# A two-layer decoder step on one core: another table of heads, kept caches and engine orders

## The chip, the core and the metric

The kernel runs on one core of one Trainium2 chip. The core has five engines that this text speaks of: PE (TensorE: matrix products), DVE (VectorE), ACT (ScalarE), POOL (GpSimd) and SP (SyncE, which here only issues DMA transfers). They run side by side and wait for each other by semaphores. The on-chip memory (SBUF) holds operands in 128 partitions; PE writes its sums into PSUM banks. The metric is the device time of one execution in microseconds (us), as the median of several runs.

## The reference

Two equal layers, each an attention block with residual and an FFN block with residual, for 4 tokens that each have their own K and V caches. Both layers use the same weights and the same caches.

```python
def _A_ref(x, k_cache, v_cache, wq, wo):          # B=4, D=448, Hq=16, Hkv=8, Dh=256, Sk=8192
    W = min(4096, max(256, Sk // 4))              # 2048: only the last 2048 positions
    q = (x @ wq).reshape(B, Sq, Hq, Dh).transpose(0, 2, 1, 3)
    k = jnp.repeat(k_cache[:, :, Sk - W:, :], rep, axis=1)      # rep = 2
    v = jnp.repeat(v_cache[:, :, Sk - W:, :], rep, axis=1)
    p = softmax(einsum("bhqd,bhkd->bhqk", q, k) * Dh ** -0.5)
    o = einsum("bhqk,bhkd->bhqd", p, v)
    return o.transpose(0, 2, 1, 3).reshape(B, Sq, Hq * Dh) @ wo
def _B_ref(x, w_gate, w_up, w_down):              # F = 1792
    return (silu(x @ w_gate) * (x @ w_up)) @ w_down

x = x + _A_ref(layernorm(x), ...)
x = x + _B_ref(layernorm(x), ...)
x = x + _A_ref(layernorm(x), ...)
x = x + _B_ref(layernorm(x), ...)
```

One token and one KV head ("a head" below) need 1 MB of K and 1 MB of V. The 32 heads of the 4 tokens are needed in layer 0 and again in layer 1, 64 heads in all. All data is bf16.

## The kernel before

**Slots and kept caches.** The weights are loaded once and stay. K and V go through 31 slots of 512 KB each, 7 more being the space of wq after its last use. A K takes two slots, a V comes in two halves with a slot each. Since both layers read the same caches, a K or a V half that the table `HOLD` names stays in its slots from layer 0 to layer 1 and is not loaded again: 21 K and 45 V halves. `SLOTS` says which slot each load takes. A load waits until the last reader of what was in its slot before has run.

**Heads and groups.** `PLAN` lists the order of the 64 heads, each as token, layer, head ("302" is token 3, layer 0, head 2). Items joined by a plus are one group of two heads, a blank parts stages, and an ampersand marks a group whose scores are made in another form (for two heads: each head's scores on their own). A group (`group`, L859) goes through: loads of K (L875 as one of 1 MB, where `WHOLE` names the head, or L881 as two halves) and of V (L897); a transpose of each K half on DVE (L887, only when the K has just been loaded); the expanded q on POOL (L926); scores on PE (L920); the maximum on DVE (L936), two small products on PE that spread it (L941, L944), its negative (L950); the exponential on ACT (L954); a turn of the probabilities on PE (L969) and their copy (L978); the totals (L986, L992); the products with V (L1001); scaling (L1015, L1017, L1019); a flip of the result (L1025, L1035). Two groups are in flight on most buffers.

**Out-projection, FFN and norm.** The out-projection (`out_proj`, L1039) adds each head to a sum in one PSUM bank, by rows (L1055, four matmuls) for all but the last head of a token and layer, and by columns (L1047) for the last; `rows` (L793: ACT copy L794, DVE subtract L796, PE turn L804, DVE add L808) brings the row sums into column form, and `residual` (L811) adds the column sums. After a token's last head come norm (L551), FFN and norm, and in layer 0 the token's q-projection for layer 1 (`qproj`, L598). The FFN has two forms. By columns (`ffn`, L711): 112 matmuls for gate and up (L740) and 56 for down (L776), each of 32 columns. By rows (`ffn_row`, L658): gate and up by L678, wide row operations (L684, L686, L688), a turn (L694) and down by rows into the sum's bank (L706), followed by `rows` again. `ROWF = (1, 2)` names the tokens that take rows in layer 0; tokens 0 and 3 take columns, and the FFN at the end of layer 1 takes columns for those tokens that have waited.

**What sets the order.** The engines' orders are written out by hand as lists of numbers (`SEQ_PE`, `SEQ_DVE`, `SEQ_ACT`, `SEQ_POOL`, `SEQ_SP`). `schedule` (L237) puts the operations into these orders, adds the waits that the data needs, and inserts zero matmuls (L1137 and, when no operand has to be loaded anew, L543), each a product with zero that adds nothing to a PSUM bank, where `SEQ_PE` has a "w" with a number. A zero matmul "w" goes into the bank of the row sums, between two of its readers. An engine that waits holds all that stands behind it in its order; this holds for SP's loads as well.

## Time and profile before

The median of 3 runs is 276.81 us (276.73 to 277.32).

| | |
|---|---|
| span of the profiled execution | 277.7 us (277.67) |
| PE busy | 242.4 us, 87% |
| DVE busy | 185.0 us, 67% |
| POOL busy | 80.4 us, 29% |
| ACT busy | 62.8 us, 23% |
| read from HBM | 100.77 MB, 363 GB/s over the span |
| mean granted clock of PE | 0.984 |

"Busy" counts instructions of the engine that work on data; a matmul and the load of its weights (PEld) overlap. The span is that of one profiled execution, from its first to its last instruction; the runs are timed without the profile. In a group of instructions, "mean ns" is the time of one record, which can overlap with the next, so that a group's busy time divided by its count is the cost of one. The chain of waits is followed back from the last instruction: a "DMA" piece is time in which the chain stood for a transfer.

### The profile page before, as it was taken

To read this page: it belongs to the slowest core of one execution; us is meant where nothing else is said; L and a number is where in the kernel's file an instruction comes from. 1 tells how busy PE (TensorE), PEld (TensorE's weight loads), DVE (VectorE), ACT (ScalarE), POOL (GpSimd) and SP (SyncE) were. 2 spreads that over 40 slices of the span, in tenths; PEclk is the share of its full clock that TensorE was granted. 3 is DMA by queue.
4 is the path that set the end of the run, shared out by engine and by line. 5 is a ranking of instruction groups with operands and counts; after the bars stand their busy time and mean duration, and the time that the engine had idled before them with its cause. 6 is when DMAs were issued, how large, how long until landed. Compare 5 with 4: busy or idle time off the path is not lost.

```text
span 277.7 us, 10576 instructions
## 1 busy us (share of the span) xinstructions
PE 242.4 (87%) x4751; PEld 126.5 (46%) x4576; DVE 185.0 (67%) x574; ACT 62.8 (23%) x173; POOL 80.4 (29%) x224
## 2 busy tenths in 40 slices
PE   3997999999999887998888887979799787989995
PEld 0121232233475553544445444535455456667664
DVE  4666817735612687978857599986768757389841
ACT  0003021111112222331332333224132321232411
POOL 1160121111024221615044243133234332254350
PEclk9998899999999999999999999999989999999998
DMA  7999999999999999999999999999999998799200
GB/s 278 425 420 413 415 395 418 399 401 406 405 387 417 411 412 414 410 409 411 351 394 400 414 417 411 408 413 408 358 384 350 411 378 297 279 396 411 81 2 3
DMA packets 25740, 101.44 MB, mean 365 GB/s; under 512 B 2523, under 2 KB 6623, under 8 KB 21471
## 3 DMA queue, kind: packets, MB, share of 16 engines
q1 hardware_dynamic: 25687, 100.78, 91.8%
q8 instruction: 36, 0.59, 0.9%
q14 instruction: 9, 0.07, 0.1%
q10 hardware_dynamic: 8, 0.00, 0.0%
HBM read 100.77 MB, written 0.00 MB: 363 GB/s over the span
## 4 chain that ended last, share of the span: by engine, by line
PE 40%; DMA 36%; DVE 14%; issue 3%; ACT 2%; SPq 2%; POOL 2%; DVEq 0%; ACTq 0%
DMA half<-in_A_v_cache_dram 24%; DMA half<-in_A_k_cache_dram 12%; DVE half L887 8%; PE S L920 8%; PE A L543 6%; PE Y L1001 6%; PE A L1137 5%; PE Z L740 3%; PE A L1055 2%; PE Z L776 2%; PE A L1047 1%; PE Y L969 1%; SPq L521 1%; DVE oh L1019 1%; SPq L897 1%
## 5 line engine op out<-in xcount | busy, mean ns | idle before, releaser
L887 DVE STREAM_TRANSPOSE half<-half 128x1024 uint32<-128x1024 uint32 x86 | 104.7, 1229 | 8.8 <-DMA half<-in_A_k_cache_dram 8.8
L1137 PE MATMUL A<-identb,small 128*128 128x512 bf16 x139 | 53.3, 389 | 3.3 <-DVE A L447 2.9
L1015 POOL TENSOR_TENSOR small<-small 128x2 f32<-128x2 f32 (+1 forms) x48 | 38.5, 805 | 47.1 <-DVE small L992 29.7
L543 PE MATMUL A<-identb,small 128*128 128x512 bf16 x175 | 51.8, 397 | 0.0
L920 PE MATMUL S<-half,qe 128*8 128x128 bf16 (+1 forms) x1520 | 45.0, 240 | 6.6 <-issue 2.8
L1001 PE MATMUL Y<-half,pT 128*8 128x256 bf16 (+1 forms) x1024 | 42.9, 274 | 8.4 <-DMA half<-in_A_v_cache_dram 5.0
L920 PEld LDWEIGHTS S<-half,qe 128*8 128x8 bf16 x1520 | 30.5, 84 | 22.3 <-DVE half L887 9.8
L954 ACT ACTIVATE praw<-S,small 104x128 bf16<-104x128 f32 (+2 forms) x48 | 19.4, 404 | 68.3 <-DVE small L950 64.1
L1019 DVE SCALAR_TENSOR_TENSOR oh<-oh,small,Y 128x256 bf16<-128x256 bf16 x48 | 22.5, 468 | 16.9 <-ACT oh L1017 16.7
L926 POOL TENSOR_TENSOR qe<-qc,tiny 128x64 bf16<-128x64 bf16 x64 | 18.1, 294 | 43.9 <-PE S L920 35.2
L1001 PEld LDWEIGHTS Y<-half,pT 128*8 128x8 bf16 (+1 forms) x1024 | 20.2, 84 | 23.0 <-DVE small L992 6.5
L1017 ACT ACTIVATE oh<-Y 128x256 bf16<-128x256 f32 x48 | 18.4, 383 | 45.8 <-PE Y L1001 37.3
L1137 PEld LDWEIGHTS A<-identb,small 128*128 128x128 bf16 x139 | 14.6, 105 | 14.9 <-issue 8.9
L577 POOL TENSOR_SCALAR st<-st 128x1 f32<-128x1 f32 x16 | 4.3, 267 | 57.6 <-DVE st L567 56.4
L978 ACT ACTIVATE pT<-Y 128x64 bf16<-128x64 f32 (+1 forms) x48 | 12.4, 258 | 36.0 <-PE Y L969 29.6
L1055 PE MATMUL A<-wo_sb,oT 128*4 128x448 bf16 x192 | 17.5, 356 | 2.0 <-issue 1.1
L1082 POOL MEMSET oT<- 128x16 bf16 x39 | 4.1, 112 | 38.4 <-PE A L1055 32.1
L992 DVE TENSOR_REDUCE small<-Y 128x2 f32<-128x32 f32 (+1 forms) x48 | 9.1, 189 | 8.8 <-PE Y L986 7.9
L1035 DVE TENSOR_TENSOR oT<-Y,small 128x4 bf16<-128x4 f32 (+1 forms) x63 | 9.0, 155 | 5.8 <-PE Y L1025 4.5
L950 DVE TENSOR_REDUCE small<-S 104x1 f32<-104x32 f32 (+1 forms) x48 | 8.5, 177 | 5.2 <-PE S L944 5.0
L941 PE MATMUL S<-small,identb 104*104 104x32 bf16 (+1 forms) x48 | 10.0, 208 | 1.9 <-DVE tiny L936 1.5
L1025 PEld LDWEIGHTS Y<-tiny,oh 128*128 128x128 bf16 x96 | 7.0, 98 | 9.6 <-DVE oh L1019 4.9
(139 smaller groups left out, 266.9 us busy)
## 6 DMA issues: line engine op xcount, KB each, us to landing
half<-in_A_v_cache_dram SPq DMA_DIRECT2D x83, 512.0 KB, 9.9
half<-in_A_k_cache_dram SPq DMA_DIRECT2D x30, 1024.0 KB, 11.2
half<-in_A_k_cache_dram SPq DMA_DIRECT2D x26, 512.0 KB, 8.9
wo_sb<-in_A_wo_dram SPq DMA_DIRECT2D x8, 448.0 KB, 17.2
half<-in_A_wq_dram SPq DMA_DIRECT2D x3, 1024.0 KB, 8.5
wd_sb<-in_B_w_down_dram SPq DMA_DIRECT2D x1, 1568.0 KB, 18.3
wg_sb<-in_B_w_gate_dram SPq DMA_DIRECT2D x1, 1344.0 KB, 18.0
wu_sb<-in_B_w_up_dram SPq DMA_DIRECT2D x1, 1344.0 KB, 20.8
```

The source lines that it names most:

```text
L543: return e.add_instruction(mybir.InstMatmult(start_tensor_calc=start, stop_tensor_calc=stop, ldweights=load, name=nc.get_next_instruction_ ...
L887: return e.transpose(a, a)
L920: last = e.matmul(Sb[s_][qd:qd + 8, 0:32 * 2 * J], lhsT=qe[q_][:, P, ce, :, :].rearrange("p a n -> p (a n)"), rhs=keys(kcs[P], J * x, J, c ...
L926: g.op(POOL, "qe", lambda e, P=P, t=t, kvh=kvh: e.tensor_tensor(qe[q_][:, P, :, :, :], qc[t][:, kvh, :, :].unsqueeze(2).broadcast_to([128, ...
L954: return e.activation(praw[0:R, 0:N].rearrange("p (g r l) -> p g r l", g=J, l=2), Sb[s_][0:R, 0:N].rearrange("p (l g r) -> p g r l", l=2, ...
L978: g.op(SCA, f"pt{n}", lambda e: e.activation(pf, Yb[p_][:, 0:PW], ACT.Copy), r=(f"yp{p_}",), w=(f"pT{pt}",), bank=(f"Y{p_}",))
L1001: last = e.matmul(Yb[p_][32 * gg:32 * gg + M, 256:512], lhsT=pT[pt][:, gg, 2 * a + hv, 4 * P:4 * P + M] if n == 2 else pf[:, 16 * gg + 8 * ...
L1015: g.op(POOL, f"pow{n}", lambda e: e.tensor_tensor(ri[p_][:, 0:2 * n], rs[p_][:, 0:2 * n], expo[:, 1:1 + 2 * n], op=ALU.pow), r=(f"rs{p_}", ...
L1017: g.op(SCA, "oh", lambda e: e.activation(oh[:, :], Yb[p_][:, 256:512], ACT.Copy), r=(f"y{p_}",), w=("oh",), bank=(f"Y{p_}",))
L1019: g.op(DVE, "oho", lambda e: e.scalar_tensor_tensor(out=oh[:, :], in0=oh[:, :], scalar=lomask[:, 0:1], in1=Yb[p_][:, 256:512], op0=ALU.mul ...
L1055: last = e.matmul(Ab[32 * k:32 * k + B, 0:D], lhsT=oT[oi][:, k % 2, k // 2, :], rhs=wo_sb[:, 4 * kvh + k, :], start=False, stop=False, ski ...
L1137: return e.matmul(Ab[:, 0:512], lhsT=w, rhs=rhs, start=False, stop=False, skip_group_check=True)
```

## The change

The tables are new, and three pieces of code with them.

- `HOLD` keeps 25 K and 44 V halves. SP issues 145 loads and one store where it issued 157 and one.
- `PLAN` has 46 stages and 55 groups (9 of two heads, 46 of one) where it had 38 and 48 (16 and 32). In layer 0 of a token, heads that are not kept come first and heads that are kept later; in layer 1 those that need a reload come at the end.
- 78 transposes instead of 86, 295 zero matmuls instead of 314. 10 of them stand behind the last matmul of the program.
- The FFN of token 1 in layer 0 is "mixed": gate and up by rows, down by columns. Tokens 0, 2 and 3 take columns (token 2 together with token 0 of layer 1). For this the down product by columns moves out of `ffn` into `ffn_down`, and `ffn_row` calls it when asked for a column result. No FFN makes its down product by rows any more, and `rows` is called 8 times instead of 10.
- Zero matmuls can go into a second bank, `Z2`: "z" with a number in `SEQ_PE`.

```diff
-ROWF = (1, 2)
+ROWF = ()
+MIXF = (1,)
 PLAN = (
-    "005+001", "002+000", "006", "007", "003+004", "101 102", "100", "017+015", "016&014", "107 013", "103 105",
...
+    "006 001", "004", "005&007", "002 003&", "000&", "100 101", "015", "013&", "016+012", "014&", "103&", "104",
...
+    "215&", "110 111", "317", "312+315", "310+313", "314+316", "211+311", "210",
 HOLD = (
...
+    "k00 k02 v020 v021 k03 v030 v031 k04 v040 v041 k05 v050 v051 k06 v060 v061 k07 v070 v071 k12 v121 k13 v130 v131 "
...
-    def schedule(self, filler):
+    def schedule(self, filler, filler2):
         real = len(self.ops)
         inA = [o for o in self.ops if o.eng != PE and "A" in o.bank]
+        inZ, on_pe = [], True
+        for o in self.ops:
+            if "Z2" in o.bank:
+                if o.eng != PE and on_pe:
+                    inZ.append([])
+                if o.eng != PE:
+                    inZ[-1].append(o)
+                on_pe = o.eng == PE
+        inZ = inZ[[z[0].kind for z in inZ].index("qc"):]
...
-                if x[0] == "w":
+                if x[0] == "z":
+                    o, k = Op(len(self.ops), PE, "fw", filler2), int(x[1:])
+                    for d in inZ[k]:
+                        o.deps[d] = True
+                    for d in inZ[k + 1] if k + 1 < len(inZ) else ():
+                        d.deps[o] = True
+                    self.ops.append(o)
...
-        def ffn_row(ts):
+        def ffn_row(ts, column=False):
...
+            if column:
+                return ffn_down(ts, lambda fc: hT[:, 16 * (fc % 4) + 4 * (fc // 4):][:, span(ts)], ("wb", "wd"))
...
+            ffn_down(ts, lambda fc: hc[:, n * fc:n * fc + n], WIDE + ("wd",), end)
+
+        def ffn_down(ts, col, r, end=False):
+            n, sl = len(ts), span(ts)
+            rep = 32 // n
+            cw = n * rep
...
-                        last = e.matmul(block(Zb, cc), lhsT=wd_sb[:, fc, c0:c0 + 128],
-                                        rhs=more(hc[:, n * fc:n * fc + n]), start=(k == 0), stop=(k == 4 * NFC - 1),
-                                        skip_group_check=True)
+                        last = e.matmul(Zb[:, cw * cc:cw * cc + cw].rearrange("p (r t) -> p r t", t=n),
+                                        lhsT=wd_sb[:, fc, c0:c0 + 128],
+                                        rhs=col(fc).unsqueeze(1).broadcast_to([128, rep, n]), start=(k == 0),
+                                        stop=(k == 4 * NFC - 1), skip_group_check=True)
...
+                    elif t in MIXF:
+                        ffn_row(with_ + [t], True)
                     else:
                         ffn(with_ + [t])
...
-        def filler(e):
+        def filler(e, bank=Ab):
...
-        g.schedule(filler)
+        g.schedule(filler, lambda e: filler(e, Z2))
```

Three places of the engines' orders show what the tables move. Line numbers shift by some 16 to 27 in the new file: scores L920 become L947, values L1001 become L1028, K loads L875 and L881 become L902 and L908, V loads L897 become L924, gate and up L740 become L758, down L776 becomes L801, the out-projection L1047 and L1055 become L1074 and L1082, zero matmuls L1137 and L543 become L1166 and L559, the turn of rows L804 becomes L831, the norm's products L561 and L569 become L577 and L585.

SP's order from the end of token 3's layer 0 to the end of the program, before (the last load of the first row is token 3's last V half of layer 0):

```order
L897 DMA half<-in_A_v_cache_dram 128x2048 x5
L881 DMA half<-in_A_k_cache_dram 128x2048
L897 DMA half<-in_A_v_cache_dram 128x2048 x3
L881 DMA half<-in_A_k_cache_dram 128x2048 x2
L897 DMA half<-in_A_v_cache_dram 128x2048 x2
L881 DMA half<-in_A_k_cache_dram 128x2048
L897 DMA half<-in_A_v_cache_dram 128x2048 x3
L881 DMA half<-in_A_k_cache_dram 128x2048 x3
L897 DMA half<-in_A_v_cache_dram 128x2048
L881 DMA half<-in_A_k_cache_dram 128x2048 x4
L897 DMA half<-in_A_v_cache_dram 128x2048 x4
```

And of the change (the tenth load of the first row is token 3's last V half of layer 0):

```order
L924 DMA half<-in_A_v_cache_dram 128x2048 x11
L902 DMA half<-in_A_k_cache_dram 128x4096
L924 DMA half<-in_A_v_cache_dram 128x2048
L908 DMA half<-in_A_k_cache_dram 128x2048 x2
L924 DMA half<-in_A_v_cache_dram 128x2048 x3
L908 DMA half<-in_A_k_cache_dram 128x2048
L924 DMA half<-in_A_v_cache_dram 128x2048
L908 DMA half<-in_A_k_cache_dram 128x2048
L902 DMA half<-in_A_k_cache_dram 128x4096
L908 DMA half<-in_A_k_cache_dram 128x2048
L924 DMA half<-in_A_v_cache_dram 128x2048
L908 DMA half<-in_A_k_cache_dram 128x2048
```

Each row of 128x2048 is one half (512 KB) a load, each of 128x4096 is a whole K. Three rows follow: a V half, a whole K and 7 V halves. Behind token 3's layer 0 there were 24 halves, and there are 27.

PE's order at the FFN of token 3 in layer 0, before, between its gate and up products and its q-projection:

```order
L920 MATMUL S<-half,qe_58 8x256 x16
L986 MATMUL Y<-pT_65,tiny 128x32
L776 MATMUL Z<-wide,wd_sb 128x32 x56
L1025 MATMUL Y<-tiny,oh 128x2 x2
L1001 MATMUL Y<-half,pT_65 4x256 x16
L561 MATMUL Z<-st,small 128x2
L920 MATMUL S<-half,qe_58 8x256 x16
L569 MATMUL Z<-xn,twice 128x1
```

And of the change, from its gate and up products to its down product:

```order
L758 MATMUL Z<-xn,wg_sb 128x32 x42
L758 MATMUL Z<-xn,wu_sb 128x32 x42
L1028 MATMUL Y<-half,pT_65 4x256 x8
L758 MATMUL Z<-st,wu_sb 128x32 x14
L758 MATMUL Z<-st,wg_sb 128x32 x14
L947 MATMUL S<-half,qe_59 8x128 x32
L968 MATMUL S<-small,identb 104x32
L971 MATMUL S<-identb,small 104x32
L801 MATMUL Z<-wide,wd_sb 128x32 x56
```

Before, a split score (8x256 x16) and a totals product stood ahead of the down product; now a whole score of one head (8x128 x32) and its spreads do.

PE's order from the last group's products with V, before:

```order
L1001 MATMUL Y<-half,pT_65 8x256 x32
L561 MATMUL Z<-st,small 128x2
L804 MATMUL Z<-tiny,wide 128x1 x8
L1137 MATMUL A<-identb,small 128x512
L543 MATMUL A<-identb,small 128x512 x2
L1025 MATMUL Y<-tiny,oh 128x4 x2
L1137 MATMUL A<-identb,small 128x512
L543 MATMUL A<-identb,small 128x512
L1047 MATMUL A<-oT_67,wo_sb 128x1 x16
L1047 MATMUL A<-oT_68,wo_sb 128x1 x16
```

And of the change:

```order
L1028 MATMUL Y<-half,pT_64 4x256 x8
L1052 MATMUL Y<-tiny,oh 128x4 x2
L1028 MATMUL Y<-half,pT_64 4x256 x8
L1074 MATMUL A<-oT_68,wo_sb 128x2 x16
L1166 MATMUL Z<-identb,small 128x512
L559 MATMUL Z<-identb,small 128x512 x2
L1052 MATMUL Y<-tiny,oh 128x2 x2
L1166 MATMUL Z<-identb,small 128x512
L577 MATMUL Z<-st,small 128x2
L1166 MATMUL Z<-identb,small 128x512
L831 MATMUL Z<-tiny,wide 128x1 x8
L1074 MATMUL A<-oT_67,wo_sb 128x1 x16
```

The last group has one head instead of two, its values stand in pieces, and the out-projection by columns of two tokens (128x2 x16) now stands ahead of the turn of the other token's rows (L831).

More of the change, by code (lines that the diff above doesn't have):

```diff
@@ L775, in down @@
                     for fc in range(NFC):
[L776 to L778 removed]
+                        last = e.matmul(Zb[:, cw * cc:cw * cc + cw].rearrange("p (r t) -> p r t", t=n),
+                                        lhsT=wd_sb[:, fc, c0:c0 + 128],
+                                        rhs=col(fc).unsqueeze(1).broadcast_to([128, rep, n]), start=(k == 0),
+                                        stop=(k == 4 * NFC - 1), skip_group_check=True)
                         k += 1
                 return last
[L781 removed]
+            g.op(PE, "downc", down, r=r, w=("z",), bank=("Z",))
+            once = Zb[:, 0:4 * cw].rearrange("p (f x) -> p f x", x=cw)[:, :, 0:n]
             if end:
[L783 removed]
+                vec("fx", lambda e: e.tensor_tensor(xb[:, :, sl], xr[:, sl, :].rearrange("p t c -> p c t"), once,
                                                     op=ALU.add), ("z",) + tuple(f"x{t}" for t in ts),
@@ L789, in ffn @@
                     vec("fx", lambda e, j=j, t=t, x=x: e.tensor_tensor(
-                        x[:, t, :], x[:, t, :], once(Zb, 4)[:, :, j],
+                        x[:, t, :], x[:, t, :], once[:, :, j],
                         op=ALU.add), ("z", key), (key,), ("Z",))
@@ L1131, in build @@
                     store()
-        def filler(e):
+        def filler(e, bank=Ab):
             w, rhs = zero[:, 0:1].broadcast_to([128, 128]), identb[:, :].unsqueeze(1).broadcast_to([128, 4, 128])
             if g.before == "fw":
-                return raw_mm(e, Ab[:, 0:512], w, rhs, (128, 128), (0, 0), False, False, False)
-            return e.matmul(Ab[:, 0:512], lhsT=w, rhs=rhs, start=False, stop=False, skip_group_check=True)
-        g.schedule(filler)
+                return raw_mm(e, bank[:, 0:512], w, rhs, (128, 128), (0, 0), False, False, False)
+            return e.matmul(bank[:, 0:512], lhsT=w, rhs=rhs, start=False, stop=False, skip_group_check=True)
+        g.schedule(filler, lambda e: filler(e, Z2))
         sems = {e: es.enter_context(nc.semaphore(f"s_{e}")) for e in (PE, DVE, SCA, POOL)}
```

7 lines of the change are left out of this document (3 added, 4 removed), and 173 rows, old and new, of tables (HOLD, PLAN, SEQ_ACT, SEQ_DVE).

## The prediction

> **What bounds the kernel now.** I read the page's slices first, then its DMA queues, then busy time by stage, then the chain of waits.
>
> ```profile
> DMA  7999999999999999999999999999999998799200
> GB/s 278 425 420 413 415 395 418 399 401 406 405 387 417 411 412 414 410 409 411 351 394 400 414 417 411 408 413 408 358 384 350 411 378 297 279 396 411 81 2 3
> q1 hardware_dynamic: 25687, 100.78, 91.8%
> ```
>
> The stream of weights and caches fills 36 of 40 slices and dips at slices 33 to 35; after slice 37 it is over. Two limits follow each other: the stream, and a last stretch of about 13 us without it. The stages, cut where token 3 turns from layer 0 to layer 1:
>
> ```profile
> 4.00:125.00 121.00, 110.82 (x1725) 45.29 (x1576) 72.54 (x216) 21.50 (x59) 28.16 (x73) 0.99 1.03 410
> 125.00:224.80 99.80, 85.37 (x1922) 48.74 (x1908) 77.86 (x219) 28.30 (x79) 34.15 (x97) 0.98 1.01 396
> 224.80:245.20 20.40, 17.14 (x422) 11.94 (x420) 11.17 (x44) 5.06 (x14) 5.40 (x19) 1.00 0.85 312
> 245.20:264.20 19.00, 18.15 (x432) 12.94 (x424) 17.20 (x54) 6.16 (x16) 7.70 (x19) 1.00 0.70 280
> 264.20:277.70 13.50, 9.86 (x259) 7.51 (x253) 3.79 (x24) 1.77 (x5) 4.25 (x10) 0.91 0.01 3
> 228.00:242.00 14.00, 11.93 (x334) 9.13 (x330) 8.31 (x33) 2.24 (x7) 3.62 (x11) 1.00 0.78 281
> ```
>
> Columns: window, its length, busy PE, PEld, DVE, ACT, POOL, granted clock, DMA share, GB/s. At 410 GB/s the stream is as fast as this trace shows it over a long stretch. In 228 to 242 it makes 281: the SBUF is full, and loads wait for slots that the heads of the layer-1 token 3 free only after its FFN. It loses 14 x (1 - 281/410) = 4.4 us there. From 245 on PE is busy for 18.15 of 19 us and DVE for 17.20, so that stage is bound by work. The chain that ended last agrees:
>
> ```profile
> 240.32 1.86 PE Z L615 x32
> 246.35 12.98 DMA half<-in_A_v_cache_dram
> 259.37 1.05 PE Y L1001 x32
> 264.20 1.05 PE Y L1001 x32
> 266.99 0.79 PE A L1047 x32
> 269.65 3.02 PE Z L740 x112
> 272.95 1.59 PE Z L776 x56
> ```
>
> The stream still delivers what the values at 259.37 need. So the span is four terms, with ends in these PE rows:
>
> ```profile
> 223.73 1.05 PE L1001 MATMUL Y<-half,pT 128*8 128x256 bf16 x32
> 235.62 1.04 PE L920 MATMUL S<-half,qe 128*8 128x256 bf16 x16 [1.66 <-issue]
> 236.64 1.56 PE L776 MATMUL Z<-wide,wd_sb 128*128 128x32 bf16 x56
> 245.24 1.11 PE L920 MATMUL S<-half,qe 128*8 128x256 bf16 x32
> 264.20 1.05 PE L1001 MATMUL Y<-half,pT 128*8 128x256 bf16 x32
> ```
>
> (a) Token 3's last layer-0 values end at 223.73 + 1.05 = 224.8. (b) Its out-projection, FFN, norm and q-projection lead to its first layer-1 score at 245.2: 20.4. (c) The heads that are left, up to the last values: 19.0. (d) From there to the end: 13.5. The profiled execution took 277.67, the median of the runs is 276.81, so I take 0.9 off the sum at the end.
>
> **Term a: the stream.**
>
> ```profile
> half<-in_A_v_cache_dram SPq DMA_DIRECT2D x83, 512.0 KB, 9.9
> half<-in_A_k_cache_dram SPq DMA_DIRECT2D x30, 1024.0 KB, 11.2
> half<-in_A_k_cache_dram SPq DMA_DIRECT2D x26, 512.0 KB, 8.9
> ```
>
> Before, these are 83 + 60 + 26 = 169 halves of 512 KB (0.524 MB). The new table keeps 25 K (two halves each) and 44 V halves, 94 halves, where the old kept 21 and 45, 87. So 7 halves, 3.67 MB, are not loaded again. More counts where they stand. On SP's order, behind the last V half of token 3's layer 0, there were 24 halves and are now 27: this half is the last of the x5 before and the tenth of the x11 after. So 10 halves, 5.24 MB, fewer stand ahead of it: 5.24 / 0.410 = 12.8 us, and token 3's layer 0 ends at 212.0. That holds if the other stalls of the stream keep their total; between 125 and 224.8 its 396 instead of 410 GB/s is 3.4 us.
>
> The Trainium skill ("DMA: Bandwidth & Descriptors", Specifications) gives some 358 GB/s as HBM's limit per core; by it the same bytes would be worth an estimated 14.6 us. The row with 410 over 121 us stands against that, and I use the row.
>
> PE is the check on this. Ahead of 224.8 it is busy for about 1 + 110.8 + 85.4 = 197 us, of which much is zero matmuls:
>
> ```profile
> L1137 PE MATMUL A<-identb,small 128*128 128x512 bf16 x139 | 53.3, 389 | 3.3 <-DVE A L447 2.9 <-DVE wide L796 0.2
> L543 PE MATMUL A<-identb,small 128*128 128x512 bf16 x175 | 51.8, 397 | 0.0
> L941 PE MATMUL S<-small,identb 104*104 104x32 bf16 x47 | 9.8, 209 | 1.9 <-DVE tiny L936 1.5 <-DVE small L936 0.3
> L986 PE MATMUL Y<-pT,tiny 128*128 128x32 bf16 x64 | 9.5, 188 | 1.1 <-ACT pT L978 0.8
> ```
>
> One costs 105.1 / 314 = 0.33 us. In the part ahead some 26 fewer stand, -8.7 us. There are 55 groups instead of 48; a further group costs its two spreads and its turn and sum, between 0.4 and 0.8 us by L941 and L986, so +3 to +6 with the dearer FFN by columns inside it. PE then has 191 to 195 us of work ahead of token 3's last values. In 4 to 125 it was busy for 110.82 of 121, 91.6%, at the stream's full speed. At that share 191 to 195 need 208.5 to 213, and end at 212.5 to 217 since PE starts at 4. So the stream says 212.0 and PE 212.5 to 217. I take **213.0**, 11.8 earlier than now, with 210 (the 3.4 us of stalls shrink) and 218 (PE, or one stall like the 4.4) as ends.
>
> **Term b.** Before, PE's next work at 235.62, a half score whose K had just been turned, came after 1.66 us of idle, with the down matmuls of token 3's FFN (236.64) queued behind it and the whole chain behind those. In the new order two scores of full length stand beside those matmuls (L947 x32, one of them ahead), for heads of other tokens that have long been loaded, so the 1.66 goes. What takes its place is a group's spread and turn in the gaps of the chain; I allow 0.5. 20.4 - 1.7 + 0.5 = **19.2**; ends 18.5 (nothing in the gaps counts) and 22 (the wait comes back and the extra groups cost 1.6).
>
> **Term c.** Before, 9 heads in 5 groups; after, 10 heads in 6.
>
> ```profile
> 228.46 0.65 PE L920 MATMUL S<-half,qe 128*8 128x128 bf16 x32
> 250.53 1.04 PE L920 MATMUL S<-half,qe 128*8 128x256 bf16 x16
> L887 DVE STREAM_TRANSPOSE half<-half x8: 1201/1234/1239, 245.3 to 258.5; 128x1024 uint32<-128x1024 uint32 x8
> ```
>
> Scores before: 2 passes at 1.11 (row 245.24) and 5 split passes at 1.04, 7.4 us. After: four pairs at 1.11 and two single heads at 0.65, 5.7. One more group costs PE up to 0.8 (above), one more head's values 1.05 (row 264.20). Four zero matmuls at 0.33 stood in the stage and none stand there now: -1.3. That is -1.7 + 0.8 + 1.05 - 1.3 = -1.2 for a PE that was busy for 18.15 of 19. The sixth group, though, is one more turn of the softmax chain, with no zero matmul or split score to fill its waits, so I give the 1.2 back: **19.0**. DVE loses 2 of 8 transposes, 2.5 us, and is no bound. Ends 17 (PE's saving and part of DVE's count) and 23 (the last loads bind).
>
> Whether they bind: 27 halves behind the last V half of layer 0 need 14.16 / 0.410 = 34.5 us; from 212.5, with a stall of 3 to 4.4 like the one of 228 to 242, they land at 250 to 251. The last values run at 213.0 + 19.2 + 19.0 = 251.2. The stream is level with the work, and with half a microsecond of room.
>
> **Term d.**
>
> ```profile
> 264.23 0.54 ACT L794 ACTIVATE wide<-A 128x448 bf16<-128x448 f32 x1 [0.64 <-PE A L1055]
> 264.80 0.63 DVE L796 TENSOR_TENSOR wide<-A,wide 128x448 bf16<-128x448 f32 x1 [0.58 <-ACT wide L794]
> 265.49 0.35 PE L804 MATMUL Z<-tiny,wide 128*128 128x1 bf16 x8
> 266.83 0.94 PE L1047 MATMUL A<-oT,wo_sb 128*128 128x1 bf16 x32
> 275.36 0.85 SPq L820 DMA_DIRECT2D out_dram<-wo_sb  x1
> ```
>
> The last group has one head, its values done in pieces of 8: 16 matmuls fewer behind its sums, at 1.05 / 32 = 0.5 us. The last out-projection by columns is 16 matmuls instead of 32, -0.47. Against it, token 2's rows (L794, L796, L804: 0.54 + 0.63 + 0.35 = 1.5) stood beside the values before; now token 3's columns (L1074 `128x2 x16`) come first and the turn of the rows after them, of which up to 0.9 may be seen. 13.5 - 1.0 + 0.5 = **13.0**, ends 12.6 and 13.5 (the 0.9 and more). The 10 zero matmuls behind the output's transpose (3.3 us) lie beside the output DMAs, which at 275.36 have 2.3 us to go: nothing, or up to 2 if PE's end is awaited and its clock falls (0.91 in the last window already). They stay out of the sum, 2 in the range.
>
> The other edits carry no term: token 1's mixed FFN and the columns of tokens 0 and 2 lie ahead of 213 and are in PE's 191 to 195; the zero matmuls into the second bank cost as much as the others; wq landing later at the start is covered by K loads that come instead, as long as the stream is full from 3 us on.
>
> **The sum.** 213.0 + 19.2 + 19.0 + 13.0 = 264.2 of span, less 0.9: **263.3 us**, 13.5 less than 276.81. Its own ends, from errors that partly cancel: 260 to 267.
>
> **The rivals.**
>
> *B, the work keeps ahead everywhere and the last landing is the end.* Layer 0 ends at 210, the stream stalls only 1 for token 3: the last half lands at 209.5 + 34.5 + 1 = 245, its values take 1, the end 12.6 to 13: 258.6 to 259 of span, 258 for the runs. For it: DVE has 2.5 us less in the last stage, and PE has gaps of 14.4 in 125 to 224.8. Against: PE at 18.15 of 19 in the stage that must shrink.
>
> *C, the stalls move to earlier tokens.* More kept halves leave fewer slots that turn over: of 31, by the tables, some 7 still turn over at the end of layer 0. Then tokens 1 and 2 can stop the stream during their chains as token 3 did, at 4.4 each, or PE's order can hold it at the 217 above. One such stall is 264.2 + 4.4 - 0.9 = 267.7, two 272.1. For it: the slices with 351, 358 and 350 GB/s are such stalls already. Against: reloads of those tokens come last now, so that their chains are covered by loads of heads that are not kept.
>
> *D, the clock.*
>
> ```profile
> 193.00:200.30 7.30, 5.16 (x126) 3.58 (x128) 4.95 (x14) 1.11 (x4) 2.56 (x7) 1.00 0.99 369
> 200.30:203.70 3.40, 3.40 (x45) 1.55 (x39) 2.07 (x7) 1.04 (x3) 0.80 (x3) 0.50 0.99 358
> ```
>
> After 7.3 us in which PE was busy for 71%, the granted clock was 0.50 for 3.4 us, and PE did 1.7 us less than at full clock. 26 zero matmuls fewer stand ahead of token 3; one further such fall makes 263.3 + 1.7 = 265.0, three 268.4. It has the sign of C and lies inside its range.
>
> The Trainium skill ("TensorE: Matmul & The Clock Gate", Part 1) has the clock fall to half after an idle window of about 3.4 us. By that rule no fall is due while PE has no such gap, and fewer zero matmuls cost nothing. The two rows disagree with its wording: PE did not stand idle that long ahead of 200.3, and it fell. I go by the rows and leave D its chance.
>
> *E, slower.* While token 3 goes through its chain, room for loads comes only from groups of other tokens that are not kept (the heads of tokens 1 and 2 whose scores stand in its gaps). If these free nothing until token 3's first layer-1 scores, the stream stands for all of term b, and all 27 halves come after it: 213.0 + 19.2 + 34.5 + 13.0 = 279.7, 278.8 for the runs, 2 slower. It decides from the point where the first load behind token 3's layer 0 needs a slot that token 3's own layer 1 frees. Against it: before, with 24 halves behind, the stall was 4.4 of 20.4; reloads of tokens 1 and 2 are among the new 27.
>
> That the change does not do what it says is out: SP's order has 145 loads where it had 157.
>
> **How the numbers follow.** Forecast 0.55 (260 to 267); B 0.12 (256 to 260); C with D 0.24 (266.5 to 273); 0.03 for some loss that eats nearly all (273 to 277.4); E 0.06. Faster by over 0.2% (what a measurement here can tell from no change, 0.55 us) are the first three and most of the fourth, 0.92, of which I hold back 0.02 for costs that no row shows; within 0.2%, 0.03; slower 0.07. The range that leaves out two in ten: 257.0 to 271.0, which leaves the far ends of B, C and E outside.
>
> **What would show it.** The bytes of the queue fall to 97.1 MB. Token 3's last values of layer 0 (L1028 ahead of its L1074) end near 213; if at 217 or later with PE busy for 95% or more, PE's order was the limit; if with slices under 380 GB/s between 100 and 213, C. The score beside token 3's L801 shows no wait over 1 us. The first layer-1 score of token 3 comes some 19 us later, the last values some 38 later, and 13 us remain. If the last V load is awaited for over 1 us, term c was the stream's. The forecast is wrong if the span is under 260 or over 268, and wrong in its ground if the four terms do not fall as above though the sum does.

## The result and the profile after

The changed kernel takes 298.8 us (median of 4 runs, 296.55 to 303.49) where the kernel before took 277.06 beside it: 1.077 of the time, 95% interval 1.0697 to 1.0843. It is 8% slower; 263.3 was forecast, 5% faster. Some executions of a kernel take over 1.5% longer than its fastest one; the ratios and their intervals in this text leave those out, the medians do not.

The page of the changed kernel, in the order in which the page of before was read (slices of the granted clock, of the transfer engines and of their rate; the stream's and the instructions' queue; the chain of waits by engine):

```profile
PE 260.7 (87%) x4962; PEld 133.4 (45%) x4807; DVE 181.0 (61%) x591; ACT 66.8 (22%) x192; POOL 82.4 (28%) x226
...
PEclk9999979999979999999799799997999857799999
DMA  7999999999967999988699999587999766989600
GB/s 284 425 421 413 413 409 397 397 384 406 328 254 263 361 425 408 418 332 296 237 397 389 375 376 400 214 292 289 367 392 372 280 204 221 323 271 411 266 2 3
...
q1 hardware_dynamic: 23959, 97.11, 85.2%
q8 instruction: 38, 0.62, 0.8%
...
PE 72%; DVE 9%; DMA 7%; issue 6%; ACT 2%; POOL 2%; SPq 1%; DVEq 0%
```

The bytes fell as foreseen, to 97.1 MB. But the stream now dips at every token (254, 237, 214, 204 GB/s), and the chain that ended last has 72% PE and 7% DMA. Before, that line read:

```profile
PE 40%; DMA 36%; DVE 14%; issue 3%; ACT 2%; SPq 2%; POOL 2%; DVEq 0%; ACTq 0%
```

The 7% of DMA are one piece of the chain, the wait for wq at the start (start, length):

```profile
5.61 20.65 DMA half<-in_A_wq_dram
```

No other piece of the chain stands for a transfer, where before eight pieces stood for a K or a V. The stages of the forecast, cut at the same events (token 3's last layer-0 values, its first layer-1 score, the last values):

```profile
4.00:125.00 121.00, 107.14 (x1585) 43.84 (x1469) 67.80 (x216) 21.26 (x60) 27.79 (x76) 0.97 0.98 383
125.00:241.50 116.50, 102.53 (x2202) 57.32 (x2177) 78.40 (x238) 31.76 (x95) 35.50 (x93) 0.93 0.88 334
241.50:262.90 21.40, 19.08 (x412) 12.34 (x410) 11.87 (x42) 4.77 (x13) 5.23 (x18) 0.74 0.73 246
262.90:285.90 23.00, 19.39 (x529) 13.00 (x530) 17.56 (x56) 7.25 (x20) 10.45 (x25) 1.00 0.77 289
285.90:298.35 12.45, 11.56 (x242) 6.75 (x224) 3.93 (x25) 1.77 (x5) 2.72 (x8) 1.00 0.01 3
```

Token 3's layer 0 ends at 241.5 where the forecast had 213.0. That one term holds 28.5 of the 34 us of span between forecast and result. The clock column has changed: 0.97, 0.93 and 0.74 where before had 0.99, 0.98 and 1.00. The trace's record of the clock has 34.1 us at half rate (at 41, 82, 144, 164, 202, 236 to 249 and 256), against 11.2 before, of which 4.3 are behind the last matmul.

Beside the clock, PE has a kind of wait that was small before. The view of waits for PE, before and after:

```profile
PE S L920 <- issue: 2.8, 2, 1.7
PE A L1055 <- issue: 1.1, 1, 1.1
PE Y L1001 <- issue: 0.9, 2, 0.6
```

```profile
PE S L947 <- issue: 6.1, 4, 3.7
PE Y L1028 <- issue: 5.8, 4, 2.0
PE Z L577 <- issue: 1.6, 1, 1.6
```

The columns are the total, how often, and the longest. "issue" is a wait for nothing that the profile shows: 13.5 us after, 4.8 before. The rows in time show that it falls in the middle of operations, between two matmuls that wait for no semaphore:

```profile
141.48 0.27 PE L577 MATMUL Z<-st,small 128*128 128x2 f32 x1
143.32 0.27 PE L577 MATMUL Z<-st,small 128*128 128x2 f32 x1 [1.57 <-issue]
...
163.36 0.61 PE L1028 MATMUL Y<-half,pT 128*4 128x256 bf16 x16 [1.50 <-issue]
199.88 0.38 PE L1028 MATMUL Y<-half,pT 128*4 128x256 bf16 x5 [1.99 <-issue]
236.30 1.01 PE L947 MATMUL S<-half,qe 128*8 128x256 bf16 x8 [3.69 <-issue]
281.16 0.52 PE L947 MATMUL S<-half,qe 128*8 128x128 bf16 x22 [1.88 <-issue]
```

By the clock's record, four of the five waits of 1.5 us or more lie beside a fall to half rate: at 143.5, 164.0 and 201.6, 0.2 to 1.7 us after PE has gone on, and at 235.7, 0.6 before it goes on. The fifth, ahead of 281.16, has none, nor has the longest of before (1.66 ahead of 235.62), and three falls (41, 82, 256) have no such wait beside them. So the waits and the falls go together often, not always. What PE waits for is in the packets of the instruction queue, the transfers ("fetches") that bring the next instructions. Counted in the trace, the waits stand between record 256k + 193 and the next of PE (matmuls, weight loads and PE's few dozen other records together), and each ends 2.2 to 2.6 us after a packet of 16 KB of that queue has started. The longest of them:

```
kernel   wait from   packet starts   PE goes on   the 256 instructions before took
before     108.46        107.45        109.80        4.96
before     215.88        214.94        217.30        5.17
before     233.89        233.36        235.62        3.92
after      141.48        140.97        143.32        5.91
after      161.78        161.14        163.36        4.20
after      180.24        179.43        181.88        4.40
after      197.62        197.58        199.88        3.49
after      232.33        233.76        236.30        4.23
after      279.06        278.62        281.16        4.74
```

So PE's program comes in blocks of 256 instructions. A block's packet starts only some time after PE has entered the block ahead of it (2.8 us in the mean before and 2.7 after; the longest after is 5.7), and PE stops where it has used up that block before the next one is there. A block lasts 6.4 us at the median before and 6.25 after, and 3.5 us where matmuls of 32 columns follow each other. The Trainium skill ("Runtime: NRT & Kernel Launch", Instruction fetch mechanics) has the same blocks of 256 and says that the fetch is mostly hidden; in this kernel it is not: PE waits 13.5 us for it.

### The profile page after: what moved, and what is told of

Its sections match the earlier page's. It is cut to its first block, busy times and chain, and to the rows that moved or that the text cites. A ratio compares the mean times of both kernels' runs of the same rounds, so it can differ in the third digit from the quotient of the medians.

```text
span 298.4 us, 11071 instructions
## 1 busy us (share of the span) xinstructions
PE 260.7 (87%) x4962; PEld 133.4 (45%) x4807; DVE 181.0 (61%) x591; ACT 66.8 (22%) x192; POOL 82.4 (28%) x226
## 4 chain that ended last, share of the span: by engine, by line
PE 72%; DVE 9%; DMA 7%; issue 6%; ACT 2%; POOL 2%; SPq 1%; DVEq 0%
PE S L947 14%; PE Y L1028 12%; PE A L1166 9%; DMA half<-in_A_wq_dram 7%; PE A L559 6%; PE Z L758 4%; PE A L1082 4%; PE Z L631 4%; DVE half L914 4%; PE Y L996 3%; PE Z L801 3%; PE Y L1052 2%; PE S L968 2%; PE Y L1013 1%; PE Z L1166 1%
## 5 line engine op out<-in xcount | busy, mean ns | idle before, releaser
L914 DVE STREAM_TRANSPOSE half<-half 128x1024 uint32<-128x1024 uint32 x78 | 95.3, 1231 | 1.6 <-DMA half<-in_A_k_cache_dram 1.5
L1042 POOL TENSOR_TENSOR small<-small 128x2 f32<-128x2 f32 (+1 forms) x55 | 41.2, 753 | 64.2 <-DVE small L1019 61.9
L947 PE MATMUL S<-half,qe 128*8 128x128 bf16 (+1 forms) x1552 | 48.7, 240 | 9.3 <-issue 6.1
L1028 PE MATMUL Y<-half,pT 128*4 128x256 bf16 (+1 forms) x1024 | 49.7, 284 | 6.7 <-issue 5.8
L1166 PE MATMUL A<-identb,small 128*128 128x512 bf16 x123 | 48.3, 403 | 2.9 <-DVE A L463 2.6
L559 PE MATMUL A<-identb,small 128*128 128x512 bf16 x146 | 44.0, 402 | 0.1
L947 PEld LDWEIGHTS S<-half,qe 128*8 128x8 bf16 x1552 | 31.5, 85 | 23.4 <-issue 9.8
L1046 DVE SCALAR_TENSOR_TENSOR oh<-oh,small,Y 128x256 bf16<-128x256 bf16 x55 | 25.8, 470 | 13.9 <-ACT oh L1044 13.1
L981 ACT ACTIVATE praw<-S,small 104x128 bf16<-104x128 f32 (+2 forms) x55 | 22.4, 408 | 50.4 <-DVE small L977 48.2
L1028 PEld LDWEIGHTS Y<-half,pT 128*4 128x4 bf16 (+1 forms) x1024 | 18.1, 83 | 23.6 <-issue 12.5
L1166 PEld LDWEIGHTS A<-identb,small 128*128 128x128 bf16 x123 | 13.0, 105 | 16.7 <-issue 11.3
L1082 PE MATMUL A<-wo_sb,oT 128*4 128x448 bf16 x204 | 18.3, 363 | 0.7 <-DVE oT L1062 0.5
L963 DVE TENSOR_REDUCE small<-S 104x1 bf16<-104x128 f32 (+2 forms) x27 | 9.2, 340 | 7.1 <-PE S L947 6.6
L963 DVE TENSOR_REDUCE tiny<-S 104x1 bf16<-104x128 f32 (+2 forms) x28 | 9.1, 326 | 6.8 <-PE S L947 6.7
L1052 PEld LDWEIGHTS Y<-tiny,oh 128*128 128x128 bf16 x110 | 7.2, 100 | 12.8 <-issue 5.5
```

The costliest lines, as they stand in the source:

```text
L559: return e.add_instruction(mybir.InstMatmult(start_tensor_calc=start, stop_tensor_calc=stop, ldweights=load, name=nc.get_next_instruction_ ...
L914: return e.transpose(a, a)
L947: last = e.matmul(Sb[s_][qd:qd + 8, 0:32 * 2 * J], lhsT=qe[q_][:, P, ce, :, :].rearrange("p a n -> p (a n)"), rhs=keys(kcs[P], J * x, J, c ...
L963: g.op(DVE, "max" + m_, lambda e: e.tensor_reduce(pmax[s_][0:R, :], Sb[s_][0:R, 0:N], AX.X, ALU.max), r=(f"s{s_}",), w=(f"pmax{s_}",), ban ...
L981: return e.activation(praw[0:R, 0:N].rearrange("p (g r l) -> p g r l", g=J, l=2), Sb[s_][0:R, 0:N].rearrange("p (l g r) -> p g r l", l=2, ...
L1028: last = e.matmul(Yb[p_][32 * gg:32 * gg + M, 256:512], lhsT=pT[pt][:, gg, 2 * a + hv, 4 * P:4 * P + M] if n == 2 else pf[:, 16 * gg + 8 * ...
```

## The experiments

The theories: **P**, PE's own order sets the pace and the stream waits for it. **S**, the stream sets the pace through slots that come free late (the forecast's view, and its rival C). **F**, instruction fetches stand in line with the stream's traffic; PE's waits for them and the half clock behind them are what is lost. All ratios are to the kernel before on the same chip.

### The start: wq ahead of the K loads

```diff
-    "50 47 196 118 167 141 49 48 191 164 51 ...      (SEQ_SP)
+    "50 47 49 48 196 51 118 167 141 191 164 ...
```

> The changed kernel with one edit: the loads of wq stand ahead of all but the first K again, so wq is complete after 5.2 MB of the stream instead of 9.4. Theory P (PE's own order sets the pace from the first q-projection on, and the stream waits for it): the first q-projection moves from 24.5 to some 15 to 18 us, token 0's out-projection by columns from 78.7 to about 73, and the end by the same 6: 291 to 294 us. Theory S (the stream sets the pace, its stalls being the slots that come free late): as many bytes in the same slots, so the lag comes back at the first stall: 297 to 300.

306.1 us, 1.091 (1.081 to 1.100) where the changed kernel has 1.077 (1.070 to 1.084): not faster, against both expectations. The edit moved the first K behind three parts of wq, and DVE's order has that K's transpose ahead of the norms' subtractions. The first score came at 39.9 instead of 34.6, the reverse of what was meant. The end came 4 us later by the ratios and 7 by the medians, with overlapping intervals and a lower clock (0.928), so this run does not tell whether a late start is absorbed.

### A light stream, in both kernels

```diff
-                        ... e.dma_start(unit(cell), vsrc[hv]), None,
+                        ... e.dma_start(
+                            unit(cell)[:, 0:HALF // few(cell)], vsrc[hv][:, 0:HALF // few(cell)]), None,
     (few is 4 for a slot that held another unit before, else 1; K loads alike)
```

> The changed kernel with a light stream: every load into a slot that has held something else before moves only a quarter of its bytes (the rest of the slot keeps the old head's data, so the attention is computed from mixed data). Orders, waits and instructions are the same; about 46 MB move instead of 97. Theory P: 285 to 299, since PE's order takes as long without a stream behind it. Theory S: 265 or less. Theory F (instruction fetches delayed by the stream make PE's 'issue' waits of 1.4 to 3.7 us, and the half clock that follows them costs as much again): the waits go away, the clock rises from 0.943 to 0.97 or more, 278 to 288.

> The same lightening of the stream in the kernel before. Its chain of waits has 36% DMA, so every theory expects it to fall; how far says how long its orders take by themselves. P: 250 to 262, far below the changed kernel's light run, since the changed orders are the longer ones. S: both light runs within 5 us of each other.

Attention is computed from mixed data in both; all instructions and waits are there. The changed kernel falls to 276.95 (ratio 0.996, 0.992 to 1.000), the kernel before to 264.6 (0.957, 0.953 to 0.961). Stages of the changed kernel's light run, up to its first score, to token 3's last layer-0 values, and to the end; then those of the kernel before:

```profile
4.00:34.60 30.60, 24.93 (x144) 4.32 (x74) 19.11 (x76) 2.66 (x3) 6.35 (x21) 1.00 1.02 418
34.60:224.00 189.40, 177.59 (x3642) 95.46 (x3572) 126.67 (x379) 50.09 (x151) 56.70 (x148) 0.98 0.46 157
224.00:273.90 49.90, 46.56 (x1177) 31.08 (x1162) 33.07 (x123) 13.68 (x38) 18.31 (x50) 1.00 0.21 61
```

```profile
4.00:28.00 24.00, 20.83 (x121) 3.82 (x74) 14.29 (x69) 2.55 (x3) 6.31 (x19) 1.00 1.01 420
28.00:212.30 184.30, 172.07 (x3524) 89.59 (x3411) 135.23 (x366) 47.15 (x135) 55.86 (x151) 1.00 0.53 185
212.30:262.70 50.40, 44.94 (x1105) 32.19 (x1092) 32.21 (x121) 12.99 (x35) 17.50 (x47) 0.98 0.31 108
```

With a stream at 157 to 185 GB/s PE is busy for 93 to 94% of the middle stage in both kernels: the orders themselves are as full as they get. The new order ends 11.2 us later in these two profiles. Its first score comes 6.6 later (34.6 against 28.0), the middle takes 5.1 longer, and the end is 0.5 shorter. No "issue" wait is left among PE's rows in either, and the mean delay of a fetch is 1.0 and 1.1 us instead of 2.7 and 2.8. The changed kernel keeps two of its falls of the clock (at 41 and 82, 6.8 us) and loses the five from 143 on. P alone had 285 or more for the changed kernel, S 265 or less: both miss, and F's 278 to 288 is the nearest, a little high. For the kernel before P had 250 to 262, and S had both light runs within 5 us of each other: neither holds, they are 12.3 apart.

### The same traffic with nobody waiting for it

```diff
+        for i in range(32):                        (16 in the second run)
+            o = g.op(SCA, "st", lambda e, i=i: e.dma_start(side[i]..., wd_sb[:, :, :]), r=("wd",))
```

> The light version of the changed kernel (276.95) with traffic beside it that nothing waits for: 32 stores of w_down from its place in SBUF to a side buffer, 1.6 MB each, issued by ACT, one after every fourth of its instructions from about 80 us on, 51 MB in all. Theory F (a fetch of instructions stands in line with whatever the transfer engines carry): the issue waits come back to 6 to 14 us, the clock falls under 0.97, and 285 to 298 us although every K and V lands early. Theory S (the gap of 22 between full and light is the stream that K and V wait for): 277 to 280, with ACT's 32 issues as the only cost.

> The light version of the changed kernel with half the side traffic, 16 stores of 1.6 MB, one after every eighth instruction of ACT. With 32 stores PE also waited 13.8 us for K and V that stood behind them. Theory F: with 16 these waits fall under 6 us, and issue waits of 3 to 7 us with a clock of 0.95 to 0.98 stay: 281 to 292. Theory S: the issue waits come only with a stream that stops PE anyway: under 2 us of them, 277 to 280.

These two add stores to the light version. With 32 of them it takes 315.1 us (1.134, 1.125 to 1.144): waits for instructions are back at 9.9 us and the clock is 0.908, but PE also waits 13.8 us for transfers that stand behind the stores, so that run (F had 285 to 298) tells nothing apart. With 16 it takes 288.9 (1.040, 1.032 to 1.048). The waits of PE there, of the light version with 16 stores:

```profile
PE S L955 <- issue: 5.0, 4, 2.9
PE Z L859 <- DMA wo_sb<-in_A_x_dram: 2.0, 1, 2.0
PE Y L1036 <- issue: 1.2, 1, 1.2
PE Z L633 <- DMA half<-in_A_wq_dram: 1.0, 1, 1.0
PE Y L1036 <- DMA half<-in_A_v_cache_dram: 0.3, 1, 0.3
```

Waits for K and V are 0.3 us, waits for instructions 6.2, the clock 0.958 instead of 0.988. The longest of them is inside the score that also waited in the changed kernel (231.18, 2.87 us; there 236.30, 3.69). Its three waits of over 1 us end at 171.5, 178.7 and 231.2, and each has a fall of the clock 0.8 to 2.5 us behind it (173.9, 180.7, 232.0) where the light run has none. The out-projections by columns stand where the light run has them up to 157 us (157.1, there 157.4), though stores move from 110 on; the next one, behind the first two of these waits, is 7.2 us late (187.5, there 180.3), and the end 13.8 in these two profiles. So traffic that gates nothing costs 12 us. F stands, with every number that it gave for this run (3 to 7 us of waits, a clock of 0.95 to 0.98, 281 to 292), and S as an explanation of the 22 us falls.

### Packets of 2 KB, in both kernels

```diff
+        def cut(e, dst, src):
+            return [e.dma_start(dst[:, c:c + 1024], src[:, c:c + 1024]) for c in range(0, dst.shape[1], 1024)]
...
-                        ... e.dma_start(unit(cell), vsrc[hv]), None,
+                        ... cut(e, unit(cell), vsrc[hv]), None,
     (K loads alike)
```

> The changed kernel, each load of K and V cut along its columns into transfers with 2 KB per partition (a whole K has 8 KB, a half 4 KB); same bytes, slots, orders. Theory F (PE runs dry because the fetch of its next block of instructions, 16 KB for 256 instructions, stands behind packets of the stream): smaller packets ahead of a fetch make its start earlier than the mean 2.7 us after the block before is used up; PE's 'issue' idle falls from 13.5 us to under 5, the clock rises above 0.97, 280 to 288 us. Rival G (the delay goes with the number of packets or the load of the memory, not with the size of packets): 297 to 303, issue idle as before.

> The same cut in the kernel before, whose 'issue' idle is 4.8 us. F: 271 to 275. G: 277 to 280.

The changed kernel takes 298.0 (1.075, 1.070 to 1.080), the kernel before 293.0 (1.059, 1.054 to 1.065). The rate of the stream falls; the kernel before with 2 KB:

```profile
GB/s 203 401 405 386 388 384 387 386 383 385 401 384 389 385 385 386 385 385 385 362 335 384 385 386 386 385 384 384 375 380 384 386 387 252 343 384 385 119 2 3
```

At 385 instead of 410 GB/s its 100.8 MB need 16 us more, and it loses 15.5; F had 271 to 275 and its rival 277 to 280. The changed kernel does not get slower by the same cut. So the kernel before is paced by its stream, and the changed one for the most part is not. The delay of a fetch stayed at 2.7 us in the mean: it does not go with the size of the packets, and F's version of this experiment (280 to 288) falls. The waits for instructions in the changed kernel went down to 3.3 us all the same without a gain: waits for DVE rose from 15.6 to 20.7 and for transfers from 2.9 to 5.0, and the half clock stayed at 34 us. Whether the slower stream took back what those 10 us would have given, or they were worth less than their length, this run does not tell.

### Where the blocks end, in the kernel before

```diff
+                if 30 < len(raws) <= 103:          (50 in the second run)
+                    for c in range(0, 512, 128):
+                        last = raw_mm(e, Ab[:, c:c + 128], w, identb[:, :], ...)
```

> The kernel before with 73 of the early zero matmuls (512 columns) made as four of 128 columns each, the same columns in all: 219 instructions more on PE ahead of about 80 us, so that every later block of 256 instructions ends 219 instructions earlier in the program. Theory F: by the times of PE's instructions in the trace of before, blocks shorter than 5.8 us (2.7 to 3.5 of delay and 2.3 from the fetch's start to PE going on) lack 6.6 us in all before, and 1.3 with the blocks moved so: issue idle falls from 4.8 to under 2.5, 273 to 276 us. If the place of the blocks does not matter: 276.5 to 278.

> The same with 20 zero matmuls cut, 60 instructions more: the blocks end where the trace of before has its densest stretches, and lack 10.1 us instead of 6.6. Theory F: issue idle 7 to 10 us, 279 to 284 us. If the place of the blocks does not matter: 276.5 to 278, as in the run beside it.

279.8 and 278.4 us (1.004, 1.000 to 1.008; 1.005, 1.002 to 1.008). The waits for instructions went the way that the place of the blocks says, 2.9 us in the first and 5.9 in the second, where 4.8 stood before, though less far than F had them. The time did not follow: both are half a per cent slower, where F had a gain for the first and 279 to 284 for the second. That a kernel paced by its stream covers 1 to 2 us of such waits, more or fewer, is the likely reason.

### Without zero matmuls from token 0's FFN on

```diff
-    ... z1 309 w4 318 317 385 w4 w4 362 319 w4 ...   (SEQ_PE, the changed kernel)
+    ... 309 318 317 385 362 319 ...
```

> The changed kernel without its 132 zero matmuls from token 0's FFN on (those of the start stay). They take 132 x 0.33 = 43 us of PE's time. Theory P: PE is the pace, so a good part comes back unless the clock takes it: 280 to 294 with the granted clock over 0.92. If the zero matmuls hold the clock and stand in gaps: the clock falls to 0.85 or less and the time rises to 300 to 315. Theory S: the same 298 to 300, whatever the clock does.

> The kernel before without its 148 zero matmuls from token 0's FFN on, as in the run on the changed kernel. There PE was the pace and 8 us came back. If before is paced by the stream with room on PE: no gain, 277 to 285, the clock at 0.85 to 0.92. If its PE order is the pace too: 265 to 272.

> The light version of the changed kernel without its 132 zero matmuls from token 0's FFN on. Nothing but PE's order, the other engines and the clock is left. If the zero matmuls stand in the path where nothing disturbs PE, it falls below the light run's 276.95: 262 to 272, with a clock of 0.88 or more. If they only fill waits, the half clock costs more than they do: 280 to 288.

The changed kernel gains: 290.7 (1.041, 1.029 to 1.052), although its clock is 0.889; P had the time, but with a clock over 0.92. The kernel before loses: 284.7 (1.026, 1.019 to 1.033), clock 0.844, about as put for a kernel that its stream paces. The light version of the changed kernel takes 281.1 with a spread from 276.1 to 283.5 around the 276.95 with zeros, which tells no gain and no certain loss. The three fit together with F and not with P as it was put: where nothing disturbs PE, its zero matmuls fill waits and cost nothing, so that the 8 us gained with the full stream are not their 43 us of work. What went is the waits for instructions, from 13.5 to 0.9 us:

```profile
PE Y L992 <- issue: 0.5, 1, 0.5
PE S L967 <- issue: 0.2, 1, 0.2
PE A L1070 <- issue: 0.2, 1, 0.2
```

218 records fewer are on PE (4830 matmuls and 4721 weight loads instead of 4962 and 4807), and none of its blocks now runs out for longer than 0.5 us. That this, and not another effect of the missing zeros, made the 8 us is argued from these rows.

### The zero matmuls at the very end

```diff
-    ... w25 w25 w25 w25 w25 w25 w25 w25 w25 w25"
```

> The changed kernel without the 10 zero matmuls behind the last matmul. They end at 297.96 of a span of 298.35 in its trace. If they lie beside the output's transfers, as the prediction had it: no change, 298 to 299.5. If the program's end waits for PE: 1 to 2 us less.

298.6 us (293.4 to 300.6): no difference that the spread of this kernel lets one see.

### Another start

```diff
-    ... 169 70 78 22 45 77 23 43 142 25 6 24 31 198 80 88 143 119 38 120 87 26 90 ...   (SEQ_DVE)
+    ... 70 78 22 45 77 23 43 25 6 24 31 80 88 38 87 26 90 119 120 142 143 ...
     (wq ahead in SEQ_SP, 19 of the first "w1" dropped in SEQ_PE)
```

> The changed kernel with another start: wq's loads ahead of all K but two, the transposes on DVE behind the first norms, and 19 of the zero matmuls between the norms left out, so that the first q-projection should begin near 18.5 instead of 24.5 and the first scores near 29 instead of 34.6. If PE's order is the pace throughout, the 5 to 6 us stay to the end: 291 to 294. If later waits take them back: 297 to 300.

The first score came at 29.7 instead of 34.6. 296.7 us (1.055, 1.043 to 1.067), from 291.0 to 299.9: 2 us less than the changed kernel by the medians, 6 by the ratios. But the early start is not what was kept. Token 0's out-projection by columns stood at 80.1, behind the 78.7 of the changed kernel: the clock was at half from 35.7 to 49.4, where the changed kernel has 3.4 us of it. The one at 190.1 is still behind the changed kernel's 188.5; this trace pulls ahead only from there on, where it has no fall of the clock (the changed kernel has three, 20.5 us together). The 5 us were won and given back by 80 us; that the 19 zero matmuls had held the clock is the likely reason.

### The mixed FFN alone, on the kernel before

```diff
-ROWF = (1, 2)
+ROWF = ()
+MIXF = (1, 2)
     (the other tables as before, without the numbers of the operations that fall away)
```

> One part of the change alone: the tables of the kernel before, with the FFN of tokens 1 and 2 in layer 0 mixed (gate and up by rows, down by columns) instead of by rows; the row copy, the subtraction and the turn behind each go away. In the trace of before that copy, subtraction and turn take 0.54 + 0.63 + 0.35 = 1.5 us of each of the two tokens' chains, the down product by columns 0.7 more than by rows. If the stream's stalls of 1.2 to 1.3 us at these tokens are set by the chain: 1 to 2 us less, 275.5 to 276.5. If the stream takes it back elsewhere: 277 to 278. If PE's 84 more instructions make it run dry: 279 to 281.

284.8 us, 1.028 (1.022 to 1.034): the third outcome, and worse than priced. 56 matmuls of 32 columns with their weight loads stand where 14 stood. The rows of the kernel before with the mixed FFN, inside the down products of tokens 2 and 3:

```profile
185.97 0.99 PE L799 MATMUL Z<-wide,wd_sb 128*128 128x32 bf16 x28 [0.24 <-DVE wide L713]
188.53 0.98 PE L799 MATMUL Z<-wide,wd_sb 128*128 128x32 bf16 x28 [1.57 <-issue]
...
236.60 1.25 PE L799 MATMUL Z<-wide,wd_sb 128*128 128x32 bf16 x44
240.84 0.47 PE L799 MATMUL Z<-wide,wd_sb 128*128 128x32 bf16 x12 [2.98 <-issue]
```

A down product is cut in two by a wait for instructions, and the waits rise from 4.8 to 8.2 us, the half clock from 11.2 to 17.7. Token 3's column FFN is unchanged; its block now ends inside the down product, and PE waits 2.98 us where it waited 1.66 just ahead of it before. Token 2's is the edit itself. In this form, for two tokens, one part of the change is by itself worth a third of what the whole lost.

## Why the prediction was wrong

**Term a is the step that failed.** It stood at 213.0 and was 241.5. The prediction took the stream's 410 GB/s as the pace, 10 halves fewer as 12.8 us, and PE as a check with 191 to 195 us of work at a share of 91.6%. Of the 28.5 us, 11.0 are there with a light stream too (224.0) and 17.5 come with the full one. The two kernels as a whole divide alike: of the 21.7 us between them, 12.3 are left between their light runs. Each piece of the term failed differently.

- *The pace.* It held for the kernel before: slow its stream by 6% and it loses all of it. It did not hold for the changed kernel, whose time does not move under the same cut. Even with a light stream token 3's layer 0 ends at 224.0, 11 later than forecast. A saving of bytes gains nothing beyond what the order of the engines takes by itself, and the old orders take 264.6 us with a quarter of those loads' bytes: some 12.8 us were there to gain, where 13.5 were forecast.
- *PE's work.* Ahead of token 3's last values PE had 1 + 20.83 + 172.07 = 194 us of work in the light run of before, and 1 + 24.93 + 177.59 = 203.5 in that of the change. The prediction gave the change 2 to 6 less. It counted 26 zero matmuls less at 8.7 us and put 3 to 6 for groups and FFN. The traces have 290 and 268 zero matmuls there, 22 less, 7.4 us at its own price; the rest added about 17, by the difference of the two runs (up to 3.4 of it from two falls of the clock in the second). The largest part is a cost that the term put at nothing, the form of the scores. In the light runs they keep PE busy for 33.8 us ahead of token 3's last values before and for 40.5 after, with 1312 and 1296 matmuls. Both have 52 heads there. Before, 18 of them are scored in pairs, 30 alone in 32 matmuls of 128x128, and 4 alone in 16 of 128x256, the form of the ampersand in `PLAN`; after, 6, 29 and 17. By the prediction's own rows a pair costs 1.11 us (245.24), the first form of one head 0.65 (228.46) and the ampersand's 1.04 (250.53), which makes an estimated 33.7 and 39.9. Term c counts such passes in its own stage; term a does not.
- *The start.* "wq landing later at the start is covered by K loads" was wrong: the first score came 5.3 us later in the full runs, 6.6 in the light ones. The DMA piece at the start of the chain (5.61 to 26.26, wq) and DVE's transposes ahead of the norms are what the rows show of that lag. Whether it alone is worth 5 us at the end stays open: the run with a later start had a lower clock, and the one with an earlier start had lost its lead by 80 us to a clock that fell.
- *The waits for instructions and the clock.* No rival had the waits, and D had the clock alone. The prediction read the row at 235.62, 1.66 us of "issue", as a wait for a K and expected it to go; it was a fetch (its packet starts at 233.36), and its kind grew to 13.5 us. With a light stream the waits are gone and 6.8 of the 34.1 us at half clock are left. Ahead of 241.5 the rows of the changed kernel have 10.7 us of such waits, and 16.0 us at half clock that the light run does not have, in which PE does up to 8.0 less: an estimate of up to 18.7 for the 17.5 us. That other traffic alone can bring both is shown by the run with 16 stores, for 12 us; that all of the 22 us between the full and the light run are theirs is argued.

**Terms b, c and d were about right.** In the light run of the changed kernel they are 17.7, 19.75 and 12.5, where the prediction had 19.2, 19.0 and 13.0. In the full run b is 21.4 at a clock of 0.74, c is 23.0 with waits for instructions of 0.97 and 1.88 in it, d is 12.45. The zero matmuls at the end cost nothing that the spread lets one see, as put. The score beside token 3's down product waits for nothing (251.28), as foreseen. The sign for term a misled: with PE busy for 88% up to 241.5 and slices under 380 GB/s, it pointed to C.

**The rivals.** C was nearest in kind, with its "PE's order can hold it": the slices fell under 380 GB/s at every token, but the chain has no K or V on it, and a light stream brings 276.95 and not 265, which speaks for slices that follow a late PE; and 217 was far too early. D had the right mechanism for a part, at a price of 1.7 us a fall and three falls at most; there were seven stretches, one 13.7 us long, 23 us more at half clock in all than before. The Trainium skill's rule that was weighed there ("TensorE: Matmul & The Clock Gate", Part 1), an idle window of 3.4 us before a fall, does not fit here either: waits of 1.5 to 2.0 us were followed by falls within 1.7 us. E gave the right sign for a reason that did not occur: the stream did not stand for the whole of token 3's chain.

**What stays open**: how the 5.1 us by which the new middle is longer with a light stream divide between the scores, the 7 more groups and the column FFNs, of which only the mixed FFN was run by itself, in the kernel before; why the clock falls beside some of the waits and not beside others; and why a fetch starts 2.7 us late behind a full stream, if not by the size of the packets ahead of it.

No version here beats the kernel before. The nearest that computes the whole reference are that kernel itself with moved blocks, half a per cent behind.

## What to carry to other kernels

A saving of bytes is worth about the gap between the kernel and itself with a light stream, and no more; that gap can be measured with one run. Here it was 12.8 us of 277, and PE's share of 87% beside the full stream was the sign that it was small. Price every form that an operation can take: here the scores of one head take 0.65 or 1.04 us by their form. Ask of every matmul series how many instructions it is, not only how long it is: here 168 matmuls of 32 columns with their weight loads are 336 instructions in some 5 us, and a block of 256 that lasts under some 5.3 us (an estimate: the median delay of 3.0 and 2.3 to go on) is likely to stop PE beside a full stream; behind the longest delays here, blocks of up to 5.9 us did. An "issue" wait in the middle of one operation is such a stop; look for the packet of the instruction queue ahead of its end before it is put down to data.

## What the runs showed that had not been expected

- PE stops at every 256th instruction if the next block is late, and goes on 2.2 to 2.7 us after the block's packet starts, in all 13 kernels here that have such stops of 0.8 us or more. The start of the packet is delayed by 2.4 to 2.9 us in the mean beside a full stream, by 1.8 in the light run with 16 stores, and by 0.7 to 1.1 in the three light runs.
- A stream of 2 KB packets, in two to four times as many transfers, runs at 385 GB/s where 4 and 8 KB ran at 410.
- The scores of one head took 1.04 us in 16 matmuls of 128x256 and 0.65 in 32 of 128x128; 32 of 128x256, for two heads, took 1.11.
